# Two score blocks and two value blocks in one TensorE step: a change to an attention + feed-forward kernel

## The chip, the cores and the metric

The kernel runs on one core of one Trainium2 chip. The metric is the device time of one execution in microseconds (us); lower is better. Three runs of the kernel before the change are given, and one execution of it was profiled.

## The reference

Attention with eight heads over 8 batches of 576 positions, then a feed-forward layer. Half of the heads see a window of the last 32 positions (local), the other half see every 32nd position (strided). All is float32.

```python
scores = scale * np.matmul(q, k.transpose(0, 1, 3, 2))          # (8, 8, 576, 576), head_dim 64
mask_local   = (rel >= 0) & (rel < 32)                           # heads 0..3
mask_strided = (rel >= 0) & (pos[None, :] % 32 == pos[:, None] % 32)   # heads 4..7
scores = np.where(masks[None], scores, -1000000000.0)
attn = softmax(scores)
x = np.matmul(attn, v)            # to (4608, 512)
h = x @ w_in                      # (4608, 2048)
g = h * (1.0 / (1.0 + np.exp(-1.702 * h)))
out = g @ w_out                   # (4608, 512)
```

## The kernel before, in words

**The feed-forward part.** Each product of `x` with `w_in` is made from float32r pieces: a value is split into a high and a low part, and high·high, high·low and low·high are added, which gives six matmuls of 128x128 weights on 288 columns for one product (two halves of the contraction, three pairs). Batch 0 is multiplied plainly, four outputs of two units for each of eight weight tiles (`plain`, L451). Batches 1 to 7 use seven products for eight (`product`, L470; `combine`, L484, adds them up on ScalarE and VectorE and stores the result to DRAM). One product of weight tile n and kind k goes to one of six PSUM banks: `mx`, `my`, `mz`, one set for even and one for odd n. After the last batch a second stage reads the hidden values back, applies the gate and multiplies by `w_out`; it isn't touched by the change.

**Steps and sides.** The program is recorded in steps of one product each (the loop at L834). A pass is one batch: 56 steps (8 weight tiles, 7 products each), and the first pass, `plain`, has 64 units. Every other piece of work is put behind a numbered step with `side(step, function, ...)`; all engines keep the order in which it was recorded. So a table of step numbers decides what stands where in each engine's queue.

**Attention of the next batch runs inside a pass.** A batch's attention is cut into six pairs of blocks (`_pairs`, L57), three local ones ("l") and three strided ones ("s"); from batch 1 on they alternate s, l. Batch 0's six pairs come before everything else. For batch b + 1, the loop at L621 puts into pass b, for each pair: `scores` (L215: TensorE, small matmuls, into the two banks `s0` and `s1`), `masked` (L265, VectorE, out of these banks), `maxima` (VectorE), `below` (GpSimd), `exps` (ScalarE), `totals` (VectorE), `scaled` (GpSimd), `turn` (L311: four TensorE transposes into `s0`, and a ScalarE copy out of it), `values` (L321: TensorE, small matmuls into `s0` and `s1`, and at once the copies out of them). `scores` and `values` are a TensorE step of their own between two products, so there are twelve such steps in a pass, and seven passes that hold them. All pairs use the same two banks one after the other. In the TensorE array the small matmuls sit in parts: scores of an l pair in parts of 64 rows by 32 columns, scores of an s pair and values of either kind in parts of 64 by 64. A profile row names a matmul's weights in that way (`64*32`, `64*64`; `54*64` is the values of an s pair, whose 54 rows lie in a part of 64).

**Weights.** `w_in` comes in as 64-bit words; `w_scale`, `w_low`, `w_join`, `w_high` and `w_low_part` (L397 to L422) make the high and low parts of a tile, then `t_load`, `t_sums`, `t_high` and `t_low` (L429 to L443) the sums of its quarters that the seven products need. They are put behind steps of the first passes (L636 to L647).

**Batch 1's input** is made from batch 1's values by `x_sum`, `x_high` and `x_low` (L367 to L385) just before the first product that uses it, by the table at L605.

Of the kernel before, what the change touches and what calls it, by code (L numbers as in the profile page):

```python
# [9 lines left out]
F32 = mybir.dt.float32  # L10
# [16 lines left out]
U = 2  # L27
# [43 lines left out]
def attn_ffn(ctx, tc, qk, vs, weights, masks, ident, out):  # L71
# [143 lines left out]
    def scores(p, banks):  # L215
# [14 lines left out]
        for i in range(4):  # L230
            for q0, n, k0, nk in windows(kind):
                for j in range(2):
                    rows = slice(j * D, (j + 1) * D)
                    matmul(
                        banks[j][q0 : q0 + n, i * WL : i * WL + nk],
# [7 lines left out]
    def parts_of(p, banks):  # L243
# [6 lines left out]
            bank[:nq, : 4 * WL].rearrange("p (i n) -> p i n", i=4)[:, :, :nk] for bank in banks  # L250
# [14 lines left out]
    def masked(p, banks):  # L265
        nq, nk, mask, pr, heads, srcs, (nmax, _, _) = parts_of(p, banks)
# [54 lines left out]
    def values(p, banks, shared=False):  # L321

# [5 lines left out]
        for g in range(2):  # L328
            for w, (q0, n, _, nk) in enumerate(windows(kind)):
                if kind == "s":  # L330
                    n = min(n0, (w + 1) * WS) - w * WS
                for u in range(U):
                    i = U * g + u
                    o = g * n0 + (q0 if kind == "l" else w * WS)
                    for j in range(2):
# [3 lines left out]
                            banks[u][j * D : (j + 1) * D, o : o + n],  # L339
                            lhsT=v[rows, i, w, :], rhs=pt[rows, i * nq + q0 : i * nq + q0 + n],  # L340
                            start=True, stop=True,
                        )
        x = {k: xr[k].rearrange("p (g n) -> p g n", g=2) for k in ("11", "12", "21", "22")}
        for u in range(U):
            src = banks[u][:, : 2 * n0].rearrange("p (g n) -> p g n", g=2)
            copy = vector.tensor_copy if shared and u else scalar.copy
            if kind == "l":
                h, o = divmod(c + u, 3)
                copy(out=x[("11", "21")[h]][:, :, o * QL : (o + 1) * QL], in_=src)
                continue  # L350
            n, r0, half = RES[c], R0[c + u], NPOS // 2
            src = src.rearrange("p g (r t) -> p g t r", r=n)
            for k, h in enumerate(("12", "22")):
                o = x[h].rearrange("p g (t r) -> p g t r", r=STRIDE)[:, :, :, r0 : r0 + n]
                copy(out=o, in_=src[:, :, k * half : (k + 1) * half])
# [76 lines left out]
    def t_sums(i):  # L432
        b11, b21, b22, b12 = (t_view(0)[:, q] for q in range(4))
        t1, t2, t3, t4 = (t_view(1 + i % 2)[:, q] for q in range(4))
        for o, x, y in ((t1, b12, b11), (t2, b22, t1), (t3, b22, b12), (t4, b21, t2)):
            gpsimd.tensor_tensor(out=o, in0=x, in1=y, op=ALU.subtract)
# [10 lines left out]
    six = [m_banks[i][x] for x in ("mx", "my", "mz") for i in range(2)]  # L447
# [516 lines left out]
```

## Time and profile before

| | |
|---|---|
| median of three runs | 859.72 us (858.7 to 861.0) |
| profiled execution | 858.98 us |
| its span, first to last instruction | 857.0 us |
| TensorE busy | 838.0 us, 98% |
| VectorE, ScalarE, GpSimd busy | 549.7, 426.9, 490.9 us |
| mean granted TensorE clock | 0.993 |

The difference between the profiled execution and its span, 1.98 us, lies around the program. In the trace all instructions have the line of one helper (L87), so one tells them by their tiles: `mx`, `my`, `mz` and `s` are PSUM banks, `xa` holds the split input, `w` the split weights, `arena` all else. PE is TensorE, PEld its weight loads, DVE VectorE, ACT ScalarE, POOL GpSimd. `128*128 128x288` are the weights and the output of a matmul. A row of a timeline gives the start, the length, the instruction and how often it follows itself; the lengths of matmuls overlap, so the distance of two starts is what a piece of work takes.

### The profile page before, as it was taken

What the parts mean: (1) busy time and instruction counts of PE and PEld (TensorE: products, weight loads), DVE (VectorE), ACT (ScalarE), POOL (GpSimd) and SP (SyncE); (2) the same over time, 40 slices, a digit from 0 to 9 for tenths busy, and PEclk for the clock granted to TensorE, in tenths of its full rate; (3) what the DMA queues carried; (4) which work ended last, traced back from release to release, by engine and by line L of the source; (5) the groups of instructions that cost most, each with busy time, mean ns of one, the idle gap of its engine ahead of it and who ended that gap; (6) DMA issues with size and microseconds to landing.
All of it is one profiled execution on the core that took longest, in us unless ns stands there. A gap on an engine that the chain in (4) does not pass through costs nothing. (4 is left out here: it accounts for less than half of the span.)

```text
span 857.0 us, 23992 instructions
## 1 busy us (share of the span) xinstructions
PE 838.0 (98%) x9827; PEld 808.8 (94%) x9827; DVE 549.7 (64%) x867; ACT 426.9 (50%) x666; POOL 490.9 (57%) x509
## 2 busy tenths in 40 slices
PE   7899999999999999999999999999999999999997
PEld 4799898999999999999999999999999999999997
DVE  5575776965857658558577775665565565566662
ACT  4675444433444434434446564655555655655540
POOL 2233866242332342423344358999998998777760
PEclk9999999999999999999999999999999999999999
DMA  8897576576685765766768853444433433443430
GB/s 330 289 395 282 174 234 222 164 254 210 205 265 175 242 212 189 253 215 203 223 233 259 266 195 109 152 159 127 146 123 124 146 126 124 141 131 123 136 106 31
DMA packets 112239, 164.84 MB, mean 192 GB/s; under 512 B 9729, under 2 KB 88321, under 8 KB 111105
## 3 DMA queue, kind: packets, MB, share of 16 engines
q1 hardware_dynamic: 112128, 163.31, 58.5%
q8 instruction: 77, 1.26, 0.6%
q14 instruction: 34, 0.27, 0.1%
HBM read 104.55 MB, written 58.72 MB: 191 GB/s over the span
## 5 line engine op out<-in xcount | busy, mean ns | idle before, releaser
L87 POOL TENSOR_TENSOR arena<-arena 128x256 f32<-128x256 f32 (+1 forms) x302 | 332.3, 1117 | 127.3 <-ACT arena L87 54.5
L87 DVE TENSOR_TENSOR xa<-arena,xa 128x576 fp32r<-128x576 f32 (+2 forms) x100 | 158.8, 1589 | 87.6 <-ACT xa L87 56.4
L87 PE MATMUL my<-xa,w 128*128 128x288 f32 x1140 | 180.3, 300 | 0.5 <-DVE arena L87 0.4
L87 ACT ACTIVATE arena<-arena 128x1024 f32<-128x1024 f32 (+2 forms) x120 | 105.4, 878 | 125.7 <-DMA arena<-hid 93.7
L87 PEld LDWEIGHTS my<-xa,w 128*128 128x128 f32 x1140 | 158.7, 189 | 3.3 <-DVE arena L87 1.0
L87 ACT CAST xa<-arena 128x576 fp32r<-128x576 f32 (+2 forms) x102 | 115.5, 1147 | 38.2 <-PE s L87 25.1
L87 PE MATMUL mx<-xa,w 128*128 128x288 f32 x804 | 132.0, 301 | 2.5 <-DVE w L87 1.0
L87 PE MATMUL mz<-xa,w 128*128 128x288 f32 x792 | 128.4, 300 | 0.0
L87 ACT COPY arena<-mx 128x288 f32<-128x288 f32 (+1 forms) x136 | 53.7, 395 | 143.0 <-PE mx L87 107.9
L87 PEld LDWEIGHTS mx<-xa,w 128*128 128x128 f32 x804 | 113.5, 190 | 4.9 <-DVE w L87 1.3
L87 DVE TENSOR_TENSOR arena<-my,arena 128x288 f32<-128x288 f32 (+1 forms) x204 | 90.0, 446 | 41.0 <-PE my L87 39.3
L87 PEld LDWEIGHTS mz<-xa,w 128*128 128x128 f32 x792 | 110.9, 188 | 1.5
L87 POOL TENSOR_TENSOR arena<-arena,rinv 96x512 f32<-96x512 f32 (+1 forms) x48 | 49.5, 1031 | 107.6 <-DVE rinv L87 64.3
L87 DVE TENSOR_TENSOR arena<-mz,arena 128x288 f32<-128x288 f32 (+1 forms) x166 | 71.7, 441 | 51.8 <-PE mz L87 50.0
L87 ACT COPY arena<-s 128x90 f32<-128x90 f32 (+4 forms) x184 | 51.3, 340 | 82.5 <-PE s L87 82.1
L87 DVE TENSOR_TENSOR ga<-arena,ga 128x1792 fp32r<-128x1792 f32 (+1 forms) x25 | 57.4, 2297 | 51.6 <-ACT ga L87 40.6
L87 POOL TENSOR_TENSOR arena<-arena,nmax 128x432 f32<-128x432 f32 (+1 forms) x42 | 46.3, 1103 | 76.7 <-DVE nmax L87 72.7
L87 PE MATMUL mz<-w_out,xa 128*128 128x256 f32 x576 | 75.5, 280 | 0.0
L87 PE MATMUL mx<-w_out,xa 128*128 128x256 f32 x576 | 75.4, 280 | 0.0
L87 PE MATMUL my<-w_out,xa 128*128 128x256 f32 x576 | 75.3, 280 | 0.0
L87 PEld LDWEIGHTS mx<-w_out,xa 128*128 128x128 f32 x576 | 71.1, 188 | 0.0
L87 PEld LDWEIGHTS my<-w_out,xa 128*128 128x128 f32 x576 | 71.0, 188 | 0.0
(72 smaller groups left out, 1000.8 us busy)
## 6 DMA issues: line engine op xcount, KB each, us to landing
hid<-arena SPq DMA_DIRECT2D x256, 144.0 KB, 3.2
arena<-hid SPq DMA_DIRECT2D x144, 256.0 KB, 3.3
arena<-qk SPq DMA_DIRECT2D x23, 448.0 KB, 4.5
arena<-qk SPq DMA_DIRECT2D x21, 472.0 KB, 4.4
arena<-vs SPq DMA_DIRECT2D x23, 384.0 KB, 4.6
out<-arena SPq DMA_DIRECT2D x34, 256.0 KB, 2.9
raw<-w_in SPq DMA_DIRECT2D x8, 1024.0 KB, 10.1
stage<-w_out SPq DMA_DIRECT2D x16, 512.0 KB, 5.1
```

Source lines behind the costliest of these rows:

```text
L87: ins = call(*args, **kw)
```

## The change

The scores of two pairs and the values of the two pairs ahead of them now stand in one TensorE step, without a product between them; there are four such steps in a pass, of which the first has only scores and the last only values.

- The scores of the second pair go to columns 256 and up of `s0` and `s1` (argument `at`), those of the first to columns 0 to 255.
- The values go to two other banks, `v_banks`: `mx` of odd weight tiles and `mz` of even ones, the second pair's from column 216 on. These banks belong to the products too; the steps are placed where both stand empty between two uses. The copies out of them are recorded behind the step, for the first bank's two pairs ahead of the second's (`moved`).
- `turn` uses `s0` for the first pair and `s1` for the second.
- `plain` uses four banks in place of six, since the two of `v_banks` are taken.
- `w_low_part` runs on GpSimd in place of VectorE for all weight tiles but the first, and weight tiles 2 to 7 are made every 6 steps instead of every 7.
- `t_sums` is cut into four pieces, one a step, and starts 5 steps earlier.
- Batch 1's input pieces are made in another order, and its first two products are exchanged (`early_one`): kind 1 ahead of kind 0. From batch 2 on, the sums start one step later.

```diff
+        return lambda u: moved(p, u, banks[u][:, at : at + 2 * n0], shared)
...
     def w_low_part(i):
-        vector.tensor_tensor(out=lo, in0=words[i], in1=hi.bitcast(F32), op=ALU.subtract)
+        (gpsimd if i else vector).tensor_tensor(
+            out=lo, in0=words[i], in1=hi.bitcast(F32), op=ALU.subtract
+        )
...
-    six = [m_banks[i][x] for x in ("mx", "my", "mz") for i in range(2)]
+    four = [m_banks[0]["mx"], m_banks[0]["my"], m_banks[1]["my"], m_banks[1]["mz"]]
+    v_banks = [m_banks[1]["mx"], m_banks[0]["mz"]]
...
-        bank = six[1 + 2 * f if j >= 4 * FP - 2 else j % 6][:, :HALF]
+        bank = (v_banks[0] if j == 4 * FP - 4 else four[j % 4])[:, :HALF]
...
+    def block(p, q, moves):
+        for i in range(2):
+            if q is not None:
+                scores(q + i, s_banks, 256 * i)
+                load_qk(q + i + 2)
+        for i in range(2):
+            if p is not None:
+                moves[i] = values(p + i, v_banks, p < 2 * PAIRS, 216 * i)
+                load_v(p + i + 2)
+
+    def blocks_of(b, slots):
+        for g in range(4):
+            s, q = slots[g], b * PAIRS + 2 * g
+            moves = {}
+            side(s, block, q - 2 if g else None, q if g < 3 else None, moves)
+            if g:
+                for i in range(4):
+                    side(s, lambda i=i, m=moves: m[i % 2](i // 2))
+            if g == 3:
+                break
+            for i in range(2):
+                p, last = q + i, slots[g + 1]
+                side(s + i, masked, p, s_banks, 256 * i)
+                for f, d in ((maxima, 2), (below, 2), (exps, 5), (totals, 6), (scaled, 6)):
+                    side(s + d + i * (2 if f in (totals, scaled) else 1), f, p, s_banks)
+                side(last - ((3, 2) if b == 1 else (3, 1))[i], turn, p, s_banks[i])
...
-        for i in range(PAIRS if b + 1 < B else 0):
...
-            side(s + t[3], turn, p, s_banks[0])
-            side(s + t[4], values, p, s_banks)
-            side(s + t[4], load_v, p + 2)
+        if b + 1 < B:
+            blocks_of(b + 1, [at + t for t in ((3, 16, 30, 44) if b else (3, 18, 33, 48))])
...
-        at = 7 * (i - 2) + 4
+        at = 6 * (i - 2) + 4
...
-        at = HEAD - 10 + STEP * i
-        for t, f in ((-3, t_load), (0, t_sums), (6, t_high), (8, t_low)):
+        at = HEAD - 15 + STEP * i
+        for m in range(4):
+            side(at + m, t_sum, i, m)
+        for t, f in ((-3, t_load), (6, t_high), (9, t_low)):
...
-                    product(n, k)
-                    combine(n, k)
+                    early_one = n == FP and k < 2
+                    product(n, 1 - k if early_one else k)
+                    if early_one and k == 0:
+                        continue
+                    for m in range(2) if early_one else (k,):
+                        combine(n, m)
```

What this does to TensorE's queue, in the middle of a pass of a late batch. `mx_76`, `my_77`, `mz_78` are the banks of even weight tiles, `mx_79`, `my_80`, `mz_81` of odd ones, `s_82` and `s_83` the two score banks; output `64x54` are an s pair's scores, or, with `x2`, its values (`64x36 x2` too), `32x64` an l pair's scores, `64x32 x2` an l pair's values. Before:

```order
L87 MATMUL my_80<-xa,w_757 128x288 x6
L87 MATMUL s_82<-arena 64x54 x2
...
L87 MATMUL mx_76<-xa,w_874 128x288 x6
L87 MATMUL s_82<-arena 64x54
...
L87 MATMUL mz_81<-xa,w_757 128x288 x6
...
L87 MATMUL s_82<-arena 64x32 x2
...
L87 MATMUL my_77<-xa,w_874 128x288 x6
L87 MATMUL s_82<-arena 32x64
...
L87 MATMUL mx_79<-xa,w_993 128x288 x6
```

After, a step with all four blocks, the transposes and the product ahead of it, and the products behind it up to the next use of `mx_79`:

```order
L87 MATMUL s_83<-ident_sb,arena 128x96 x4
L87 MATMUL my_77<-xa,w_666 128x288 x6
L87 MATMUL s_82<-arena 64x54
...
L87 MATMUL s_82<-arena 32x64
...
L87 MATMUL mx_79<-arena 64x54 x2
...
L87 MATMUL mx_79<-arena 64x32 x2
...
L87 MATMUL my_80<-xa,w_550 128x288 x6
L87 MATMUL mx_76<-xa,w_666 128x288 x6
L87 MATMUL mz_81<-xa,w_550 128x288 x6
...
L87 MATMUL mx_79<-xa,w_724 128x288 x6
```

The four blocks that stood alone between products now follow each other, and the values have left the score banks; four products stand between the values and the next product into `mx_79` (the fourth, into `my_77`, is left out above).

GpSimd's queue where the first pass begins (`w_550`, `w_636` or `w_666`, `w_757` or `w_724` are weight tiles 1, 2, 3; `nmax` marks `below`, `rinv` marks `scaled`). Before:

```order
L87 TENSOR_TENSOR arena<-arena,nmax_577 128x4x2x54
L87 TENSOR_TENSOR arena<-arena,rinv_579 128x4x2x54
L87 TENSOR_TENSOR arena<-arena,nmax_671 96x4x128
L87 TENSOR_TENSOR arena<-arena,rinv_673 96x4x128
L87 TENSOR_TENSOR arena<-arena,nmax_784 128x4x2x54
```

After:

```order
L87 TENSOR_TENSOR w_550<-raw_121,w_550 128x4x256
L87 TENSOR_TENSOR arena<-arena,nmax_608 128x4x2x54
L87 TENSOR_TENSOR arena<-arena,nmax_623 96x4x128
L87 TENSOR_TENSOR arena<-arena,rinv_610 128x4x2x54
L87 TENSOR_TENSOR w_666<-raw_534,w_666 128x4x256
L87 TENSOR_TENSOR arena<-arena,rinv_625 96x4x128
L87 TENSOR_TENSOR w_724<-raw_542,w_724 128x4x256
```

The low parts of the weight tiles now stand among the attention work of GpSimd's queue.

More of the change, by code (lines that the diff above doesn't have):

```diff
@@ L213, in geom, with scores @@
         return nq, nk, 1, masks_sb[:nq, m, :nk].unsqueeze(1).broadcast_to([nq, 4, nk])
-    def scores(p, banks):
+    def scores(p, banks, at=0):
         kind = pairs[p][0]
@@ L241, in attn_ffn, with parts_of @@
     sums_of = {}
-    def parts_of(p, banks):
+    def parts_of(p, banks, at=0):
         nq, nk, _, mask = geom(p)
@@ L249, in parts_of @@
         srcs = [
-            bank[:nq, : 4 * WL].rearrange("p (i n) -> p i n", i=4)[:, :, :nk] for bank in banks
+            bank[:nq, at : at + 4 * WL].rearrange("p (i n) -> p i n", i=4)[:, :, :nk]
+            for bank in banks
         ]
@@ L319, in turn, with values @@
         scalar.copy(out=pts[p % 2][:, : 4 * nq], in_=bank[:, : 4 * nq])
-    def values(p, banks, shared=False):
+    def values(p, banks, shared=False, at=0):
         kind, b, c = pairs[p]
@@ L342, in values, with moved @@
                         )
+        return lambda u: moved(p, u, banks[u][:, at : at + 2 * n0], shared)
+    def moved(p, u, src, shared):
+        kind, _, c = pairs[p]
         x = {k: xr[k].rearrange("p (g n) -> p g n", g=2) for k in ("11", "12", "21", "22")}
[L344 to L355, printed above, removed]
+        src = src.rearrange("p (g n) -> p g n", g=2)
+        copy = vector.tensor_copy if shared and u else scalar.copy
+        if kind == "l":
+            h, o = divmod(c + u, 3)
+            copy(out=x[("11", "21")[h]][:, :, o * QL : (o + 1) * QL], in_=src)
+            return
+        n, r0, half = RES[c], R0[c + u], NPOS // 2
+        src = src.rearrange("p g (r t) -> p g t r", r=n)
+        for k, h in enumerate(("12", "22")):
+            o = x[h].rearrange("p g (t r) -> p g t r", r=STRIDE)[:, :, :, r0 : r0 + n]
+            copy(out=o, in_=src[:, :, k * half : (k + 1) * half])
     halves = {k: t.rearrange("p (c n) -> p c n", c=2) for k, t in xr.items()}
@@ L557, in attn_ffn @@
         if i >= 3:
-            values(i - 3, s_banks, i == n0 + 2)
+            move = values(i - 3, s_banks, i == n0 + 2)
+            for u in range(U):
+                move(u)
         if i == 4:
@@ L620, in attn_ffn @@
             side(at, x_sum, 4, b)
-        for i in range(PAIRS if b + 1 < B else 0):
-            p = (b + 1) * PAIRS + i
-            s = at + 4 + 6 * i if b > 1 else at - 3 * b + 7 * i + 2 * (not b)
-            t = (4, 5, 6, 9, 11) if b > 1 else (4, 5, 6, 11, 12) if b and not i else (5, 6, 7, 10, 12)
-            side(s, scores, p, s_banks)
-            side(s, load_qk, p + 2)
-            for f, d in ((masked, 0), (maxima, 1), (below, 2), (exps, t[0]), (totals, t[1]), (scaled, t[2])):
-                side(s + d, f, p, s_banks)
-            side(s + t[3], turn, p, s_banks[0])
-            side(s + t[4], values, p, s_banks)
-            side(s + t[4], load_v, p + 2)
+        if b + 1 < B:
+            blocks_of(b + 1, [at + t for t in ((3, 16, 30, 44) if b else (3, 18, 33, 48))])
     def word(f, i):
@@ L686, in attn_ffn @@
     for h in range(2 * FP):
-        c = first(2 + h // 3) + 9 + 14 * (h % 3) if h < 15 else last - 5
+        c = first(2 + h // 3) + 8 + 14 * (h % 3) if h < 15 else last - 5
         side(c - 8, half_load, h)
```

28 lines of the change are left out of this document (14 added, 14 removed).

## The prediction

> **What bounds the kernel now.** I read the page first, then the stretches by time.
>
> ```profile
> span 857.0 us, 23992 instructions
> PE 838.0 (98%) x9827; PEld 808.8 (94%) x9827; DVE 549.7 (64%) x867; ACT 426.9 (50%) x666; POOL 490.9 (57%) x509
> ```
>
> ```profile
> 240.00:300.00 60.00, 60.00 (x890) 57.16 (x888) 40.14 (x85) 25.93 (x63) 21.06 (x27) 1.00 0.69 220
> 300.00:360.00 60.00, 60.00 (x900) 57.07 (x892) 41.28 (x88) 24.92 (x64) 21.74 (x28) 1.00 0.68 217
> ```
>
> TensorE (PE) is busy for 98% of the span, and in the passes (columns: length, then busy us of PE, PEld, DVE, ACT, POOL, granted clock, DMA share) for all of it, at full clock, with the next engine at two thirds. So the time is what stands in TensorE's queue, and the question is what a row in it costs beyond its own columns. That is read from the distances of starts in TensorE's timeline, in the middle of a pass:
>
> ```profile
> 312.47 0.95 PE L87 MATMUL mx<-xa,w 128*128 128x288 f32 x6
> 313.36 0.67 PE L87 MATMUL s<-arena 54*64 54x54 f32 x32
> 313.96 1.07 PE L87 MATMUL mz<-xa,w 128*128 128x288 f32 x6
> 314.86 0.96 PE L87 MATMUL my<-xa,w 128*128 128x288 f32 x6
> 315.66 0.96 PE L87 MATMUL mx<-xa,w 128*128 128x288 f32 x6
> ...
> 319.29 0.90 PE L87 MATMUL s<-arena 64*64 64x32 f32 x48
> 320.12 1.06 PE L87 MATMUL mx<-xa,w 128*128 128x288 f32 x6
> 321.02 0.96 PE L87 MATMUL mz<-xa,w 128*128 128x288 f32 x6
> ```
>
> A product followed by a product takes 0.80 us from start to start (314.86 to 315.66). A product followed by attention takes 0.89 (312.47 to 313.36), and the first product behind attention 0.90 (313.96 to 314.86). The attention itself, start to next start, takes 0.60 with 32 matmuls and 0.83 with 48 (319.29 to 320.12). The 16 more cost 0.23, so one costs 14.4 ns and 32 cost 0.46; 0.14 of the 0.60 is the way out. A step of attention alone thus has a fixed price of 0.09 + 0.14 + 0.10 = 0.33 us, whatever is in it. In the waits the same shows as weight loads that wait for nothing named:
>
> ```profile
> PEld s L87 <- issue: 12.1, 73, 0.4
> ```
>
> **The change: fewer steps.** There are twelve attention steps in a pass and four after, in seven passes: 8 x 7 = 56 fixed prices fewer, 56 x 0.33 = 18.5 us. The small matmuls themselves stay, and so do the transposes; no engine that TensorE waits for hides this part, since TensorE never waits there.
>
> In place of each step removed stands a join between two blocks. Per pass there is one in the first step (s scores to l scores), three in each of the middle two, one in the last (s values to l values): 8. Three of these join parts of 64 by 64 to parts of 64 by 64 (both of the last kind, in three steps). Five have l scores, in parts of 64 by 32, on one side.
>
> The first kind stands in the trace, before the passes, where scores and values of batch 0 follow each other:
>
> ```profile
> 16.77 0.69 PE L87 MATMUL mx<-early 64*64 64x54 f32 x32 [2.32 <-DMA early<-qk]
> 17.28 0.86 PE L87 MATMUL s<-arena 64*64 64x32 f32 x48
> ```
>
> 0.51 from start to start, against the 0.46 of 32 matmuls: at most 0.05, and some of that belongs to the first block's entry. I take 0.03: 21 x 0.03 = 0.6 us.
>
> The second kind, between 64 by 64 and 64 by 32, stands nowhere in the trace. Its bounds are this cheap join, 0.03, and a whole fixed price, 0.33, since it can't need more than leaving for a product and coming back. [...] 35 x 0.14 = 4.9 us (1.1 to 11.6). [...]
>
> Together: 18.5 - 0.6 - 4.9 = 13.0 us less in TensorE's queue.
>
> **The change: new waits in the passes.** Three could arise.
>
> *Scores behind the second transpose.* The second pair's transposes are one product ahead of the next scores, which overwrite the same bank, so its copy must be out.
>
> ```profile
> 317.24 0.50 PE L87 MATMUL s<-ident_sb,arena 96*128 96x96 f32 x4
> 317.52 1.84 PE L87 MATMUL my<-xa,w 128*128 128x288 f32 x12
> ```
>
> ```profile
> 283.55 0.60 PE L87 MATMUL s<-ident_sb,arena 128*128 128x128 f32 x4
> ```
>
> ```profile
> 284.18 0.59 ACT L87 COPY arena<-s 128x512 f32<-128x512 f32 x1 [1.05 <-PE s L87]
> ```
>
> ```profile
> L87 ACT COPY arena<-s 128x384 f32<-128x384 f32 x21 | 10.1, 480 | 26.6 <-PE s L87 26.6
> ```
>
> ScalarE starts the copy 0.03 us after the transposes' end (284.15 to 284.18). For an l pair that is 0.50 + 0.03 + 0.48 = 1.01 us from their start. TensorE reaches the scores after 0.28 (317.24 to 317.52) and one product with its way in, 0.89: 1.17. A margin of 0.16 us, so no wait as long as ScalarE is free; what stands ahead of the copy is a copy of a product two earlier. I take 0 here; 0.1 in each of 14 steps would be 1.4 us.
>
> *Products behind the values.* The values lie in product banks. Each step's six copies stand together in ScalarE's queue; the first bank has to be free after four products, 4 x 0.80 + 0.10 = 3.3 us.
>
> ```profile
> L87 ACT COPY arena<-s 128x90 f32<-128x90 f32 x62 | 10.3, 259 | 9.0 <-PE s L87 9.0
> L87 ACT COPY arena<-s 128x192 f32<-128x192 f32 x48 | 13.0, 323 | 27.6 <-PE s L87 27.6
> ```
>
> Its three copies take 2 x 0.26 + 0.32 = 0.84 us: 2.4 us to spare, with ScalarE busy for 25 of 60 us. Cost 0.
>
> *VectorE's queue.* `masked` now waits for both pairs' scores, and the next sums of products stand behind it. While it waits TensorE is at the values, and the bank those sums empty is next written four products later. Cost 0.
>
> **The change: the first pass and its end.** TensorE stands still in a few places before; these rows give the idle time in brackets.
>
> ```profile
> 43.49 0.66 PE L87 MATMUL s<-ident_sb,arena 128*128 128x128 f32 x4 [0.29 <-POOL arena L87]
> ```
>
> ```profile
> 95.09 0.40 PE L87 MATMUL mx<-xa,w 128*128 128x288 f32 x1 [0.74 <-ACT xa L87]
> 96.24 0.93 PE L87 MATMUL mx<-xa,w 128*128 128x288 f32 x5 [0.75 <-DVE xa L87]
> ```
>
> ```profile
> 144.19 0.55 PE L87 MATMUL s<-ident_sb,arena 96*128 96x96 f32 x4 [1.05 <-POOL arena L87]
> ```
>
> At 95 and 96 the first product of batch 1 waits for its input, which ScalarE and VectorE make late. After the change the kind that is needed first is made first, and kind 0 has two more steps: I take both away, 1.5 us. At 43.5 and 144.2 a transpose waits for GpSimd, at 144 behind four of the weight sums in a row; these now stand one a step, and the transposes later behind their `scaled`: 0.3 gone, and half of 1.05, 0.5, since GpSimd has no less to do.
>
> Against that, weight tile 1's low part goes to GpSimd.
>
> ```profile
> L87 POOL TENSOR_TENSOR xa<-arena,xa 128x576 fp32r<-128x576 f32 x2 | 2.8, 1416 | 3.6 <-ACT xa L87 3.6
> ```
>
> ```profile
> 37.00 1.23 DVE L87 TENSOR_TENSOR w<-raw,w 128x1024 fp32r<-128x1024 f32 x1 [1.12 <-ACT w L87]
> ```
>
> ```profile
> 38.21 1.75 PE L87 MATMUL mz<-xa,w 128*128 128x288 f32 x12
> 39.89 0.74 PE L87 MATMUL s<-arena 64*32 64x64 f32 x48
> 40.55 1.86 PE L87 MATMUL mz<-xa,w 128*128 128x288 f32 x12
> ```
>
> The same subtraction on GpSimd takes 1.416 x 1024 / 576 = 2.5 us, in place of 1.23: from 37.0 to 39.5. TensorE needed the tile at 38.21, as VectorE ended; now the second pair's scores (0.66, 39.89 to 40.55) stand ahead of that, so it comes at 38.87 and waits 0.6 to 0.7. I take 0.7. For tiles 2 to 7 the lead grows by two steps a tile, since they are made every 6 steps and used every 8: cost 0. The four banks of `plain` are used again after 8 steps in place of 12, and hold a result for 3 of them; 5 products, 4 us, cover the copy. Together: 0.7 - 1.5 - 0.3 - 0.5 = -1.6 us.
>
> **The sum.** 13.0 + 1.6 = 14.6 us off the profiled execution's 858.98 (span 857.0 and 1.98 around it). That execution lies 0.74 below the median, 859.72; from the median: 845.1 us.
>
> **The rivals.**
>
> *Joins of 64 by 64 with 64 by 32 are free.* They cost 0.03 like the others: 18.5 - 56 x 0.03 + 1.6 = 18.4 us, 841.3. For it: 48 l scores take 0.66 to the next product (39.89 to 40.55), less than 48 values, so the smaller parts as such cost nothing. Against it: the way in and out of the full array shows that a change of shape can cost.
>
> *They cost a whole fixed price.* 35 x 0.33 = 11.6: 18.5 - 0.6 - 11.6 + 1.6 = 7.9, 851.8. For it: the price of a change in the trace is the same for every block. Against it: 0.19 of it belongs to the 288-column neighbours.
>
> *GpSimd late in the first pass.* If low parts of tiles 1 to 7 keep TensorE waiting 2 us each in place of 0.7 once, 13.3 us more, and the sum is nearly nil: 858.4.
>
> ```profile
> 0.00:60.00 60.00, 50.59 (x958) 41.09 (x959) 37.05 (x76) 36.38 (x69) 20.06 (x34) 0.97 0.89 332
> ```
>
> For it: seven times 2.5 us put among `below` and `scaled`, whose results the transposes need. Against it: POOL is busy for a third of the first 60 us, and the lead grows.
>
> *Slower: products wait for ScalarE to empty the value banks.* ScalarE's queue is in order; if a copy or an `exps` ahead of the six waits, all six wait, and the next product into `mx` with them. It decides from a lateness of 2.4 us, and to eat 14.6 us in 21 such steps it must be 0.7 more, 3.1 each time. At 4 us each: 21 x 1.6 = 33.6, so 878.7. For it: ScalarE waits for GpSimd and DMA in places. Against it: an `exps` stands 5 steps behind its scores, and the next value step 8 behind that.
>
> **How the numbers follow.** The forecast has 0.55, free joins 0.20, joins at full price 0.13, GpSimd late 0.07, slower 0.05. 0.3% of 859.72, 2.6 us, is about what a measurement can tell from no change; faster means below 857.1. The first three and about half of the fourth are faster: 0.92; the other half of the fourth, 0.03, is within; slower 0.05. The forecast's own range is 842 to 848; taking in free joins (841.3, with the stalls all gone down to 839) and full price (851.8, with 1.4 of scores waiting for a copy up to 853) gives 839 to 853.
>
> **What would show it.** In the profile after: the weight loads that wait on "issue" at `s` drop from 73 to about a third; a step with all four blocks takes 160 x 14.4 ns = 2.3 us, plus two joins of 0.14 and one of 0.03 and the way out 0.14, some 2.8 us to the next product; no idle brackets at steps of scores or at `mx` of odd tiles in the passes; about 0.7 us idle for POOL at the first `w` product of tile 1; none at batch 1's first product. Wrong would be: a gap over 0.3 us at l scores, `mx` or `s` waiting on ACT in each pass, or PE no longer busy at 60 of 60 us in the passes.

## The result, and the profile after

| | before | after |
|---|---|---|
| median | 860.36 us (4 runs, 858.70 to 861.14) | 866.15 us (4 runs, 862.45 to 867.74) |
| profiled execution, its span | 858.98, 857.0 us | 862.45, 860.7 us |
| TensorE busy | 838.0 us | 827.9 us |
| granted clock of the four runs after | | 0.993 (profiled), 0.984, 0.984, 0.990 |

The ratio is 1.0066, with a 95% interval of 1.0043 to 1.0089: the kernel is slower by 5.7 us, where 14.6 less was forecast. TensorE's own work did shrink, by 10 us. The page:

```profile
span 860.7 us, 23887 instructions
PE 827.9 (96%) x9827; PEld 806.5 (94%) x9827; DVE 539.4 (63%) x869; ACT 422.3 (49%) x657; POOL 501.3 (58%) x516
```

So 33 us of the span are idle for TensorE in place of 19. Where, the stretches by time tell (length; busy us of PE, PEld, DVE, ACT, POOL; granted clock; DMA share; GB/s):

```profile
120.00:180.00 60.00, 55.46 (x793) 53.57 (x794) 40.14 (x82) 23.88 (x57) 27.82 (x30) 0.97 0.63 197
240.00:300.00 60.00, 60.00 (x914) 58.74 (x907) 41.80 (x90) 25.07 (x66) 21.40 (x28) 1.00 0.71 230
360.00:420.00 60.00, 58.14 (x860) 56.58 (x859) 41.35 (x85) 24.11 (x60) 22.59 (x28) 1.00 0.66 219
```

TensorE is full in one pass and not in the next, though all passes hold the same work. For the account, the span is cut at fixed products (each 56th product starts a pass), and the starts are read from the trace:

| stretch | before | after | change |
|---|---|---|---|
| up to the first product | 28.42 | 27.97 | -0.45 |
| first pass, with the first products of batch 1 among its last | 71.00 | 74.17 | +3.17 |
| batch 1's pass | 58.93 | 65.79 | +6.86 |
| passes of batch 2, 3, 4, 5 | 57.40 each | 56.00, 56.05, 55.40, 55.98 | -6.16 |
| pass of batch 6 | 57.40 | 58.26 | +0.86 |
| batch 7 and the second stage | 411.66 | 411.05 | -0.61 |

**What came as forecast.** A pass in which TensorE waits for nothing takes 55.40 in place of 57.40. The 2.0 us stand against 13.0 / 7 = 1.86 forecast. In TensorE's timeline, a step of four blocks and the products around it:

```profile
292.48 1.04 PE L87 MATMUL my<-xa,w 128*128 128x288 f32 x6
293.45 1.35 PE L87 MATMUL s<-arena 64*64 64x54 f32 x80
...
295.87 0.23 PE L87 MATMUL mx<-arena 64*64 64x32 f32 x2
295.88 0.23 PE L87 MATMUL mz<-arena 64*64 64x32 f32 x2
296.03 1.07 PE L87 MATMUL my<-xa,w 128*128 128x288 f32 x6
```

It takes 2.58 us from its start to the next product (293.45 to 296.03), where 2.8 was expected. Inside it, the first matmul behind a join of s and l scores starts 148 ns after the last one ahead of it, and 146 ns between l scores and s values; neighbours of one kind mostly stand 6 to 39 ns apart, the last s value and the first l value 20 ns. (Three neighbours inside blocks stand 47 to 80 ns apart.) So a join of the second kind costs some 0.11 us, 148 less 38 ns (forecast 0.14), and one of the first kind nothing that can be seen (forecast 0.03). The weight loads that wait for "issue" at `s` fall from 73 to 16:

```profile
PEld s L87 <- issue: 3.2, 16, 0.5
```

**What had not been forecast.** TensorE's waits (us in total, times, the longest):

```profile
PE s L87 <- POOL arena L87: 5.4, 8, 2.2
PE my L87 <- ACT w L87: 4.5, 1, 4.5
PE my L87 <- issue: 1.9, 2, 1.5
PE mz L87 <- issue: 1.8, 1, 1.8
PE mx L87 <- issue: 1.5, 1, 1.5
PE mx L87 <- POOL w L87: 0.2, 1, 0.2
```

The last line is the wait for weight tile 1, forecast at 0.7 and 0.2 in fact. The other five come to some 15 us, of which 1.5 (transposes for GpSimd) stood there before; they have three causes. One wait outside these lines is a kind that the prediction had named: in the first pass, scores wait for ScalarE's copies of the transposes out of `s0` and `s1`.

```profile
66.05 0.97 ACT L87 COPY arena<-s 128x512 f32<-128x512 f32 x2
66.70 1.00 PE L87 MATMUL s<-arena 64*64 64x54 f32 x29 [0.81 <-ACT arena L87]
```

*Batch 1's first products.* Where two waits of 0.74 and 0.75 were to vanish, there is one of 4.53:

```profile
91.90 1.75 PE L87 MATMUL my<-xa,w 128*128 128x288 f32 x12
98.18 1.06 PE L87 MATMUL my<-xa,w 128*128 128x288 f32 x3 [4.53 <-ACT w L87]
```

GpSimd's timeline after and, below it, before. `sums` are the weight sums, `arena` 128x576 is `x_sum` 3, batch 1's input:

```profile
83.68 2.94 POOL L87 TENSOR_TENSOR sums<-sums 128x256 f32<-128x256 f32 x4 [3.33 <-issue]
91.39 0.73 POOL L87 TENSOR_TENSOR sums<-sums 128x256 f32<-128x256 f32 x1 [4.77 <-DMA sums<-plains]
92.08 1.43 POOL L87 TENSOR_TENSOR arena<-arena 128x576 f32<-128x576 f32 x1
```

```profile
86.49 3.35 POOL L87 TENSOR_TENSOR sums<-sums 128x256 f32<-128x256 f32 x4 [4.93 <-DMA sums<-plains]
89.80 1.43 POOL L87 TENSOR_TENSOR arena<-arena 128x576 f32<-128x576 f32 x1
94.03 1.54 POOL L87 TENSOR_TENSOR sums<-sums 128x256 f32<-128x256 f32 x2 [2.81 <-DMA sums<-plains]
```

Before, `x_sum` 3 stands behind tile 0's sums and ahead of tile 1's. After, the first of tile 1's sums is one step ahead of it, and waits 4.77 us for its load (there is one landing buffer, free only when tile 0's sums are made at 86.6). `x_sum` 3 stands behind it with its input ready, and ScalarE's queue behind that:

```profile
94.84 0.67 ACT L87 CAST xa<-arena 128x576 fp32r<-128x576 f32 x1 [5.46 <-DVE arena L87]
...
97.08 1.05 ACT L87 CAST w<-sums 128x1024 fp32r<-128x1024 f32 x1 [0.70 <-POOL sums L87]
```

*Transposes that wait for GpSimd*, 2.15 and 0.81 in batch 1's pass and 0.31 in most others. In GpSimd's queue the two `below` and the two `scaled` of a group stand among the weight sums:

```profile
115.95 0.66 PE L87 MATMUL s<-ident_sb,arena 128*128 128x128 f32 x4 [2.15 <-POOL arena L87]
```

```profile
107.74 5.11 POOL L87 TENSOR_TENSOR arena<-arena,nmax 128x432 f32<-128x432 f32 x2 [1.20 <-DVE nmax L87]
112.81 2.22 POOL L87 TENSOR_TENSOR sums<-sums 128x256 f32<-128x256 f32 x3
114.99 0.91 POOL L87 TENSOR_TENSOR arena<-arena,rinv 128x432 f32<-128x432 f32 x1
```

The first `scaled` ends at 115.9, and the transposes start with it. The order is not all of it: the two `below` take 5.11 us (2.09 and 3.06), where the other groups of this pass need 0.92 and 1.04. The long ones, from 107.74 to 112.85, run while VectorE subtracts the low parts of `xa` and `w` (three subtractions between 107.88 and 111.94, of 0.74, 1.29 and 1.21 us); that this is the reason was not tested.

*Waits on "issue" at steps of four blocks*, four of them, 5.1 us in all: 1.46 at 123.3 and 1.83 at 141.5 inside a step, 1.54 at 409.9 and 0.31 at 425.7 in the product right behind one. TensorE, in the middle of the values of an l pair:

```profile
121.58 0.23 PE L87 MATMUL mx<-arena 64*64 64x32 f32 x2
121.59 0.23 PE L87 MATMUL mz<-arena 64*64 64x32 f32 x2
123.28 0.25 PE L87 MATMUL mx<-arena 64*64 64x32 f32 x2 [1.46 <-issue]
123.30 0.25 PE L87 MATMUL mz<-arena 64*64 64x32 f32 x2
```

No engine, semaphore or transfer of data is named. The page has a queue for instructions:

```profile
q8 instruction: 77, 1.26, 0.6%
```

77 packets of 16 KB for the 19,711 TensorE instructions of the trace come to 256 instructions a packet, an estimate from these two counts that takes all the packets for TensorE's. Counted in the program, all four stalls lie at the same place modulo 256, instruction 226 or 227 (192 or 193 if the trace's are counted); I take this place for the cut between two such blocks. For the stall at 123.28 the packet started at 120.94, 1.66 us into the step, took 0.99 us, and TensorE went on 2.34 us after its start. The same holds for every wait on issue at such a cut in the passes of the changed kernel and of the experiments below, 33 in all: TensorE goes on 2.2 to 2.9 us after a packet of this queue starts. That TensorE waits there for the next instructions themselves is my theory, the "instruction fetch" of the expectations below; the traces show the places and the times. A four-block step is 160 matmuls with a weight load each, 320 instructions in 2.5 us, so it can meet two cuts within 2 us, less than these 2.2 to 2.9. The steps that stall start at 180, 173, 162 and 155 (modulo 256, from the program's start; the expectations below call this instructions into a block), 46 to 71 ahead of a cut, and meet the next one 302 to 327 instructions in, at their end or a few instructions behind it. Eight of the ten others end before their second cut. Two start 2 and 9 instructions ahead of the first, so that the second lies inside the step too; for them the packet starts 0.9 and 1.1 us ahead of the step, some 3 us before the second cut, and there is no wait. A step before had at most 96 instructions.

### The profile page after: what moved, and what is told of

It reads as the page before. It is cut to its first block, busy times and chain, and to the rows that moved or that the text cites. A ratio compares the mean times of both kernels' runs of the same rounds, so it can differ in the third digit from the quotient of the medians.

```text
span 860.7 us, 23887 instructions
## 1 busy us (share of the span) xinstructions
PE 827.9 (96%) x9827; PEld 806.5 (94%) x9827; DVE 539.4 (63%) x869; ACT 422.3 (49%) x657; POOL 501.3 (58%) x516
## 5 line engine op out<-in xcount | busy, mean ns | idle before, releaser
L87 POOL TENSOR_TENSOR arena<-arena 128x256 f32<-128x256 f32 (+1 forms) x302 | 323.8, 1089 | 145.8 <-ACT arena L87 67.8
L87 PE MATMUL my<-xa,w 128*128 128x288 f32 x1200 | 190.2, 300 | 8.2 <-ACT w L87 4.5
L87 PEld LDWEIGHTS my<-xa,w 128*128 128x128 f32 x1200 | 167.8, 190 | 10.5 <-ACT w L87 4.7
L87 ACT ACTIVATE arena<-arena 128x1024 f32<-128x1024 f32 (+2 forms) x120 | 104.1, 878 | 123.3 <-DMA arena<-hid 94.4
L87 ACT COPY arena<-mx 128x288 f32<-128x288 f32 (+4 forms) x201 | 67.0, 358 | 183.7 <-PE mx L87 126.1
L87 PE MATMUL mx<-xa,w 128*128 128x288 f32 x768 | 126.6, 300 | 1.2 <-DVE w L87 1.0
L87 PE MATMUL mz<-xa,w 128*128 128x288 f32 x768 | 124.1, 298 | 0.0
L87 PEld LDWEIGHTS mx<-xa,w 128*128 128x128 f32 x768 | 109.5, 190 | 2.4 <-DVE w L87 1.2
L87 POOL TENSOR_TENSOR arena<-arena,nmax 128x432 f32<-128x432 f32 (+1 forms) x42 | 50.8, 1218 | 98.9 <-DVE nmax L87 91.6
L87 DVE TENSOR_TENSOR ga<-arena,ga 128x1792 fp32r<-128x1792 f32 (+1 forms) x25 | 55.4, 2215 | 52.2 <-ACT ga L87 34.8
L87 PEld LDWEIGHTS mz<-w_out,xa 128*128 128x128 f32 x576 | 70.9, 188 | 0.0
```

Source lines behind the costliest of these rows:

```text
L87: ins = call(*args, **kw)
```

## The experiments

All kernels are the changed one or the one before, with the edit shown; the ratio is always to the kernel before, measured beside it.

### 1. Batch 1's third sum one step earlier

```
-  (-8, x_sum, 1), (-7, x_sum, 3), (-6, x_sum, 2)
+  (-8, x_sum, 1), (-8, x_sum, 3), (-6, x_sum, 2)
```

> The changed kernel with one number moved: batch 1's x_sum of kind 3 goes one step earlier, so that in GpSimd's queue it stands ahead of the first piece of weight tile 1's sums and no longer behind it. Theory 'queue order': that piece waits 4.8 us for its DMA and holds up x_sum, and with it batch 1's first product, so the 4.5 us wait of TensorE at 98 us goes, and the kernel takes 861 to 862 us against 866 of the changed kernel (before: 860). Rival 'GpSimd has too much to do in the first pass': its work is the same, the wait only moves to the next product, and the time stays at 865 to 866.

863.6 us, ratio 1.0033 (1.0012 to 1.0054). TensorE's timeline:

```profile
94.91 1.04 PE L87 MATMUL my<-xa,w 128*128 128x288 f32 x6 [0.62 <-DVE arena L87]
...
107.11 0.40 PE L87 MATMUL my<-xa,w 128*128 128x288 f32 x1 [2.55 <-ACT xa L87]
108.47 0.85 PE L87 MATMUL my<-xa,w 128*128 128x288 f32 x2 [0.96 <-DVE xa L87]
```

The wait of 4.53 falls to 0.62: the place in GpSimd's queue was its cause. But of the 3.9 us, 2.5 come back twelve microseconds later, where other parts of the same input are late: 3.5 in place of the 1.03 that the changed kernel waits there. The wait of 2.15 for GpSimd is gone; the two `below` ahead of it now take

```profile
105.37 2.43 POOL L87 TENSOR_TENSOR arena<-arena,nmax 128x432 f32<-128x432 f32 x2
```

in place of 5.11 us. The first pass and batch 1's pass together take 136.7 us in place of 140.0. The time lies between theory (861 to 862) and rival (865 to 866). The four waits on issue stay at the same steps (1.46, 1.56, 1.50, 0.06).

### 2. The weight sums where they stood before

```
-  at = HEAD - 15 + STEP * i
-  for m in range(4): side(at + m, t_sum, i, m)
+  at = HEAD - 10 + STEP * i
+  for m in range(4): side(at, t_sum, i, m)
```

> The changed kernel with the weight sums as before the change: the four pieces of a tile at once, five steps later. Theory 'queue order': the 4.5 us at 98 us go, and so do most of the waits behind them for GpSimd (1.0 at 110, 2.2 at 116, 0.8 at 133 us), since a tile's sums wait for the DMA into one landing place that the sums before them must have left, and pieces spread over steps leave it later; 857 to 860 us. Rival 'GpSimd has too much to do': low parts of the weights still stand in its queue, so over 3 us of waits for POOL stay in the first two passes and the time is 862 or more.

869.47 us, ratio 1.0098 (1.0065 to 1.0130). The theory failed: TensorE now waits 4.59 for ScalarE and 2.70 for the weights of batch 1's first products. In GpSimd's queue `x_sum` 3 now stands behind all four sums of tile 0, which wait for their load until 91.45. So the earlier place of the sums is not in itself what costs the time.

### 3. Other places in the blocks of 256

The warm-up's first 7 matmuls of 512 columns become 72 of 48: 130 instructions more ahead of everything, the columns nearly the same.

```
-  fill(FILL[i][0], late)
+  for _ in range(72):
+      matmul(late[:, :48], lhsT=zeros[:, :P], rhs=zeros[:, :48], start=True, stop=True)
```

> The changed kernel with 65 more matmuls (130 more TensorE instructions) in the warm-up at the start: 72 of 48 columns in place of 7 of 512, so that nothing changes but where the program's instructions are cut into fetches of 256. Theory 'instruction fetch': a step of four blocks is 320 instructions in 2.5 us, and where it begins some 25 to 85 instructions ahead of a cut it runs through the whole next fetch before the one after it has landed; with the shift no step begins there but one or two at the edge, and the 5.1 us of waits for 'issue' at 123, 141, 410 and 426 us go (at most 1 us in all stays, near 182, 197 or 349 us); 861 us against 866. Rival 'the steps themselves wait' (a bank, a semaphore that the profile does not show): the waits stay at the same four steps and the time at 866.

868.93 us, ratio 1.0098 (1.0065 to 1.0132): the 861 of the theory did not come. No wait on issue is left at the four steps; they now come at 186.6 and 204.4, in the pass behind, and one at 57.9 among plain products:

```profile
183.79 0.23 PE L87 MATMUL mx<-arena 64*64 64x32 f32 x2
186.65 0.25 PE L87 MATMUL mz<-arena 64*64 64x32 f32 x2 [2.63 <-issue]
```

The steps with a wait start at 204 and 197; the old ones did at 180, 173, 162 and 155. The place is as the fetch theory says; the size is not: 2.63 and 1.18, and 1.08 at 57.9, where at most 1 in all was expected. And batch 1's pass, now without its waits on issue of 3.3 us, takes 64.2, only 1.6 less, since the transposes wait for GpSimd instead, 2.15, 2.65 and 1.37 in three groups in place of 2.15, 0.81 and none. In that pass two things are late, one behind the other.

### 4. A product between scores and values

```
-  side(s, block, ...)            # scores and values
+  side(s, block_s, ...)
+  side(s + 1, block_v, ...)      # one product later
```

> The changed kernel with a product between the scores and the values of each step of four blocks: six steps a pass, none over 160 instructions. Theory 'instruction fetch': no wait for 'issue' in the passes, 5.1 us less; 14 more steps at 0.33 less a join of 0.12 each cost 2.9 us: 864 against 866. Rival 'the steps themselves wait': the waits move to the steps of values, and the time is 868 to 869.

864.37 us, ratio 1.0056 (1.0030 to 1.0083). The expected 864 came out, but not by the expected way: the waits on issue do not vanish, they become 0.43, 0.78, 1.12 and 0.19, 2.5 us in place of 5.1. A later pass takes 0.3 to 0.4 more. The wait of 4.5 at batch 1's first product stays, and those for GpSimd at transposes of batch 1's pass grow from 3.0 to 5.1. The time can't be told from that of the changed kernel.

### 5. Grouped steps from batch 2's pass on, all else as before

Kernel before, with `block` and `blocks_of` of the change for the passes of batch 2 to 6:

```
+  if 1 < b < B - 1:
+      blocks_of(b + 1, [at + t for t in (3, 16, 30, 44)])
-  for i in range(PAIRS if b + 1 < B else 0):
+  for i in range(PAIRS if b < 2 else 0):
```

> The kernel before, with the grouped steps of the change only from the pass of batch 2 on; the first pass and the pass of batch 1 are those of before. Theory one (the loss sits in the first pass and in the pass of batch 1, in the order of GpSimd's queue, and the grouped steps bring what they should, 1.4 us a pass with the wait for GpSimd at a pass's first transposes): five passes of 55.99 us in place of 57.40, so 7.0 us fewer, less about 1.5 us each for the two grouped steps that now start 187 and 180 instructions into a block of 256 (last pass with attention): some 856 us, 3 to 5 below before, and no wait over 1.1 us at batch 1's first product. Rival (the grouped steps as such are what costs, by banks, by a late ScalarE or by the clock): five passes no shorter than 57.4, 860 or more.

857.77 us, ratio 0.9968 (0.9951 to 0.9984): faster than before. The five passes take 55.40, 55.98, 56.77 (with 0.52 on issue), 55.98 and 60.13. The first has no wait for GpSimd at its transposes, so 0.31 us of that wait makes 0.6 us of a pass. The last has its two steps at 187 and 180, with waits of 2.54 and 1.13:

```profile
403.91 0.24 PE L87 MATMUL mz<-arena 64*64 64x32 f32 x2 [2.54 <-issue]
```

### 6. The side work of the change alone

Kernel before, with the change's order of weights, weight sums and batch 1's parts (the last four hunks of the diff), and its low parts on GpSimd; attention stays one block a step.

```
-  at = 7 * (i - 2) + 4
+  at = 6 * (i - 2) + 4
...
-  for t, f in ((-3, t_load), (0, t_sums), (6, t_high), (8, t_low)):
+  for m in range(4): side(at + m, t_sum, i, m)      # at is five steps earlier
+  for t, f in ((-3, t_load), (6, t_high), (9, t_low)):
```

> The kernel before with the side work of the change alone: weight tiles every 6 steps, low parts of tiles 1 to 7 on GpSimd, weight sums five steps earlier and one piece a step, batch 1's parts in the new order; attention stays one block a step. Theory one (queue order on GpSimd is the cause): batch 1's first product waits 4 us or more, as after the change, the first pass and the pass of batch 1 together take 6 to 10 us more than before, the later passes 57.4 each: 866 to 870. Rival (the grouped attention of the first two passes makes the inputs late): no wait over 1.1 us at batch 1's first product, 858 to 861.

861.45 us, ratio 1.0024 (1.0008 to 1.0039): far below the 866 of theory one, and 0.45 above the rival's range, which allowed no wait over 1.1. Batch 1's first product waits

```profile
98.20 0.40 PE L87 MATMUL my<-xa,w 128*128 128x288 f32 x1 [0.99 <-ACT xa L87]
100.36 1.01 PE L87 MATMUL my<-xa,w 128*128 128x288 f32 x5 [1.75 <-DVE xa L87]
```

2.7 us, against 1.5 before and 4.5 in the changed kernel; `x_sum` 3 stands behind a weight sum that waits 3.83 us for its load, as after the change. Batch 1's pass takes 58.90 as before. So the order alone takes the gain away that I had put down there and makes a small loss of it; most of the loss came only with grouped attention beside it.

### 7. The sum earlier, and the low parts back on VectorE

```
-  (-8, x_sum, 1), (-7, x_sum, 3)
+  (-8, x_sum, 1), (-8, x_sum, 3)
-  (gpsimd if i else vector).tensor_tensor(
+  vector.tensor_tensor(
```

> The changed kernel with batch 1's third sum one step earlier in GpSimd's queue, and the low parts of weight tiles 1 to 7 back on VectorE. Theory (GpSimd has too much queued in the first pass): 7 x 2.4 us of GpSimd's time go, the waits for POOL at transposes (116, 131, 151 us) and for xa at 107 fall under 0.5 us each, and the time falls 3 to 5 us below the 863.6 of the run with the sum moved alone: 859 to 861. Rival (VectorE is the late engine at the end of the first pass): the waits for DVE at xa grow past 1 us, 863 or more.

864.88 us, ratio 1.0063 (1.0042 to 1.0083), not the 859 to 861 of the theory and no better than experiment 1: the waits for GpSimd at transposes are eleven now, 5.7 us together, and the two for `xa` are 2.95 and 0.96. So seven low parts on GpSimd are not why its results come late. The rival has the time right; the wait for VectorE that it named, over 1 us, stays at 0.96.

### 8. Experiment 5 at another place, and transposes one step later

```
-  side(last - (3, 1)[i], turn, p, s_banks[i])
+  side(last - ((2, 1) if g == 0 else (3, 1))[i], turn, p, s_banks[i])
+  118 warm-up matmuls of 30 columns in place of 7 of 512
```

> As the kernel with grouped steps from batch 2's pass on, with two edits more: the first group's transposes one step later for its first pair, which should take away the wait of 0.31 us for GpSimd, worth 0.6 us a pass; and 111 matmuls of 30 columns more in the warm-up in place of 7 of 512, which move all later instructions by 222, so that the ten grouped steps start 65, 58, 215, 208, 109, 102, 3, 252, 153 and 146 instructions into a block. Theory (a step that starts some 155 to 205 into a block overtakes the fetch): no wait on issue over 0.4 us but perhaps one of up to 1 at 208; five passes of 55.4: 850 us, 9 to 10 below before. Rival (waits on issue belong to the last grouped pass, not to the place in the block): two of about 1.5 us at 410 and 426 us as in the changed kernel, 853 or more.

855.34 us, ratio 0.9946 (0.9926 to 0.9966). 850 us were expected. The waits for GpSimd in the grouped passes are gone, and passes without a wait on issue take 55.4 to 55.5, as expected. The two waits left the last pass's two steps, as expected too; but two came elsewhere, 1.73 in the step that starts at 208, and 1.84 some products behind the one at 153. Each is followed by a lower granted clock. Ahead of the first wait, around it, and behind it:

```profile
244.00:247.00 3.00, 1.86 (x118) 1.60 (x111) 0.78 (x3) 0.00 (x0) 0.00 (x0) 1.00 0.84 252
247.00:252.00 5.00, 4.40 (x40) 4.36 (x40) 1.62 (x4) 1.49 (x7) 0.62 (x1) 0.66 0.72 257
252.00:256.00 4.00, 4.00 (x32) 4.00 (x32) 2.66 (x7) 2.08 (x5) 1.34 (x2) 1.00 0.50 188
```

A clock of 0.66 over 5 us is 3.4 us at half speed, 1.7 us lost; half speed is what the clock shows after the change, 0.50 from 142.5 to 145.9. So this pass takes 59.01, 3.6 more than 55.4: 1.73 of wait and 1.7 of clock.

### 9. No grouped step between 143 and 208

As 8, with 124 matmuls in the warm-up (of 28 columns, to keep their sum; 234 instructions more than experiment 5), and a product between scores and values in the last pass alone, whose steps would start at 165 and 158.

```
+  apart = int(b == B - 1 and 0 < g < 3)
+  side(s, block, None if apart or not g else q - 2, q if g < 3 else None, moves)
+  if apart: side(s + 1, block, q - 2, None, moves)
```

> Grouped steps from batch 2's pass on, the first pair's transposes one step later in the first group, and two edits against the waits on issue: 117 matmuls of 30 columns more in the warm-up in place of 7 of 512 (all later instructions move by 234), so that the grouped steps start 77, 70, 227, 220, 121, 114, 15 and 8 instructions into a block, outside the 143 to 208 where waits were seen; in the last pass with attention, where they would start at 165 and 158, a product stands between scores and values, as in the run with all steps split. Theory (place in the block of 256): no wait on issue in the first four of the five passes, 55.4 us each; about 1.3 us of waits and 0.3 for the split in the last, so 10.0 - 1.6 = 8.4 us below before, 850 to 852.5. Rival (the waits come in some pass or other whatever the place): two of 1.5 us or more, and a slower clock behind them, as with 111 matmuls: 855.

853.03 us, ratio 0.9913 (0.9891 to 0.9934): the fastest kernel here, 7 us below before, where 8.4 was expected. In the eight unsplit grouped steps there is no wait on issue; the first four grouped passes take 55.40, 55.76, 55.47 and 55.47, with TensorE full:

```profile
220.00:280.00 60.00, 59.98 (x874) 58.64 (x874) 44.01 (x90) 25.42 (x64) 23.38 (x28) 1.00 0.70 228
280.00:340.00 60.00, 60.00 (x878) 58.77 (x877) 44.12 (x92) 26.41 (x66) 24.02 (x30) 1.00 0.67 221
```

In the last, 59.74, the split did not help. A clock at half speed for 3.4 us, from 402.5 on (the product at 402.49 takes 1.42 us to the next start, where 0.80 is usual), adds 1.7 us to this wait:

```profile
401.36 0.24 PE L87 MATMUL mx<-arena 64*64 64x32 f32 x1 [1.55 <-issue]
```

### 10. The changed kernel, batch 1's pass alone ungrouped

```
-  if b + 1 < B:
+  if b + 1 < B and b != 1:
       blocks_of(...)
+  # for b == 1: the loop of before, one block a step
```

> The changed kernel, with the pass of batch 1 alone back to one block a step (its slots of before); the first pass and passes 2 to 6 stay grouped, the side work stays that of the change. Theory (grouping in that pass costs 6.9 us: two fetch waits of 1.5 and 1.8, two waits for GpSimd at transposes of 2.2 and 0.8, the rest of it clock and late parts): the pass takes 59 to 60.5 in place of 65.8, the wait of some 4.5 us at batch 1's first product stays, and so do about 3 us of waits on issue in the last pass with attention: 859 to 861.5. Rival (the late inputs of batch 1 delay the pass whatever is in it): the pass 63 or more, 864 or more.

860.72 us, ratio 1.0003 (0.9984 to 1.0023). The pass takes 58.43 in place of 65.79, better than expected, though the late input is still there in front of it:

```profile
100.44 0.89 PE L87 MATMUL my<-xa,w 128*128 128x288 f32 x4 [3.84 <-ACT xa L87]
```

Waits for GpSimd at transposes in that pass come to 0.6 us in place of 3.0, and there are none on issue. The last grouped pass has 2.23 and 1.47 on issue (steps at 171 and 164).

### 11 and 12. The side work in two parts

Kernel before with the low parts of tiles 1 to 7 on GpSimd and nothing else (11), and with all the side work of experiment 6 but that (12).

```
11:
-  vector.tensor_tensor(
+  (gpsimd if i else vector).tensor_tensor(
12: experiment 6 with this line as before
```

> The kernel before with one edit of the change: the low parts of weight tiles 1 to 7 on GpSimd. As predicted, one wait of 0.7 to 0.9 us for tile 1 and nothing else: the first pass 72, 860.5 to 862. Rival (7 x 2.4 us on GpSimd hold up the transposes and the sums of batch 1): the first pass 73.5 or more, with waits for POOL beyond those of before, 863 or more.

859.68 us, ratio 0.9997 (0.9980 to 1.0014), just below the expected 860.5 to 862, and a first pass of 70.50. The wait that was expected is there:

```profile
41.58 0.67 PE L87 MATMUL mz<-xa,w 128*128 128x288 f32 x3 [0.88 <-POOL w L87]
```

> The kernel before with the side work of the change (weight tiles every 6 steps, weight sums earlier, batch 1's parts in the new order) but the low parts left on VectorE. Theory (batch 1's third sum stands behind weight sums that wait for a DMA): the waits at batch 1's first two products come to 2.5 us or more, against 1.5 before, and none for a weight tile at 41 us; 860.5 to 862. Rival (the low parts on GpSimd were what made them late): waits of 1.5 or less, 858.5 to 860.

860.79 us, ratio 1.0009 (0.9992 to 1.0025); waits of 0.96 and 1.76 at batch 1's first products, 2.7 in all, as in experiment 6. Neither part can be told from no change in the time; the wait of 0.9 belongs to the low parts, that of 2.7 to the order.

## Why the prediction was wrong

**The account.** From the ratios: grouping in passes 2 to 6 makes -2.8 us (experiment 5), the side work alone +2.1 (6), the changed kernel without grouping in batch 1's pass +0.3 (10), with it +5.7. The difference of the last two, +5.4, is the price of grouping in batch 1's pass, and what is left, 0.3 + 2.8 - 2.1 = +1.0, that of grouping in the first pass. This adds up by construction, and each term has an uncertainty of 1 to 2 us. Against the forecast, by the stretches of the profiled executions: the passes of batch 2 to 6 are 4.0 us longer than forecast (-5.3 against 5 x -1.86), batch 1's pass 9.2 (+6.86 against -1.86 - 0.5) and the first pass with its end 6.1 (+3.17 against -1.86 - 1.1). That is more than the 18.3 us between -14.6 and +3.7, since the start and the second stage came out 1.1 shorter.

**Fewer steps and joins: right.** 18.5 - 5.5 = 13.0 us was forecast for seven passes, 1.86 each; a clean pass gains 2.0. The prices were near: some 0.11 and 0 a join for 0.14 and 0.03. The 0.14 is the price measured for the way out of a step; no run of before shows it for a join of 64 by 64 with 64 by 32. After the change the starts at those joins stand 146 and 148 ns apart, against 6 to 39 at most others, which gives the 0.11; why they cost this was not shown. Neither the rival of free joins nor that of full-price joins decided anything.

**"New waits in the passes. Three could arise": this step failed.** The three cost nothing in the steady passes: no scores wait for the copy of the transposes in the passes of batch 2 to 6, and VectorE's queue holds up nothing there. The first of them arose once, in the first pass: 0.81 us at 66.7. Its condition, a free ScalarE, does not hold there: ScalarE is at the weights until 65.9 and at the two copies from 66.05 to 67.02. No product in any pass waits for the value banks, so the rival that ended on the slower side named a wait that isn't there. What cost most was not among the three. The prediction priced a step by the distances of TensorE's starts and put waits on issue at nothing: they came to 5.1 us, with 1.7 of half-speed clock (0.50 from 142.5 to 145.9) behind one of them. In the changed kernel and experiments 1 to 3, 5 and 7 to 10 there are 110 unsplit four-block steps. All 23 that start at 155 to 208 have a wait, 0.06 to 2.63 us, inside the step or in the first product behind it; of the other 87 none does. Four of those, which start at 123, 142, 143 and 153, have a wait one to three products behind (1.08, 0.10, 0.52, 1.84). Moving the program's instructions moves the waits (3, 8), and keeping the steps out of that part leaves eight steps without any (9). That is shown. That TensorE waits there for its instructions is not: it is my reading of the 256 instructions a packet and of the packet that starts 2.2 to 2.9 us ahead of TensorE's going on, each time, and no experiment changed the packets themselves.

**The 0.31 for GpSimd in the passes** (0.6 us a pass, four passes, 2.4 us) was missed as well: the argument looked at the banks behind the transposes and not at `scaled` ahead of the first one. One step later it is gone (8).

**"Together: 0.7 - 1.5 - 0.3 - 0.5 = -1.6 us" for the first pass and its end: this step failed too.** The 0.7 was near (0.21 in the changed kernel, 0.88 alone). The 1.5 to be taken away at batch 1's first product became a wait of 4.5: the prediction looked at the order of the parts among themselves, and not at the weight sums that had been moved past them in GpSimd's queue, nor at the load those wait for. Experiment 1 shows that cause, and also that curing it alone brings 2.5 of the 3.9 us back elsewhere. The 0.3 that the first pass's transposes were to lose came the other way: they wait 1.18 for GpSimd, where 0.50 stood before. The transposes behind weight sums wait 3.0 in batch 1's pass, where 1.05 stood before and half of it was to remain: the sums stand one a step now, but the two `below` and two `scaled` of a group have to pass them together, where before each had its own steps. How much of the 3.0 that order makes is open, since the first group's two `below` alone took 3.2 us longer than usual, more than the 2.15 of wait behind them; where they took 2.43 (experiment 1) that wait was gone. The rival "GpSimd late in the first pass" had the right engine and the wrong reason: experiments 7 and 11 show that the low parts are not it.

**What stays open.** In batch 1's pass the waits named come to 3.3 on issue and 4.0 for GpSimd and the input, less the 1.05 of before; half-speed clock costs 1.7 (at 142) against 0.8 before (the end of a stretch from 97.6 to 101.0), and 2.0 is the gain: 5.2 of the 6.86 us. The rest is not in gaps, of which the profile shows only 0.1 us more in that pass. It may be that a wait costs more than its gap, as the 0.31 at transposes makes 0.6 of a pass. How the price of that pass divides between the waits on issue and GpSimd is not settled: with the 3.3 on issue taken away (3), the waits for GpSimd at transposes grew from 3.0 to 6.2, and the pass became shorter by 1.6, about the 1.7 of half-speed clock that is not in it. How long a stall lasts at the same place of a block goes with when its packet starts: in experiment 5's last pass 2.63 us into the step for the wait of 2.54, and 0.96 for that of 1.13. Why the packet starts early or late was not found out, and so neither why the split in experiment 9 left 1.55 where in experiment 4 it left 0.2 to 1.1.

## What to carry to other kernels

Before many small instructions are put in one run, count them: here a run of 320 instructions in 2.5 us had a wait on issue of 0.06 to 2.63 us, inside it or right behind it, wherever it began 18 to 71 ahead of a cut between blocks of 256 (23 of 23), and one such wait could take back what a pass had gained. Where work is moved in an in-order queue, look at every instruction it now stands ahead of, and at what it itself waits for: one weight sum of 0.7 us that waits 4.77 us for a load held up batch 1's whole input. And change a steady stage before a crowded one: the same grouping that gains 2 us in each steady pass lost 5 in the pass in which GpSimd also makes the weight sums, by late inputs and waits on issue together.

## What the hardware showed that I had not expected

- A wait of TensorE of 1.5 to 2.6 us, in or behind a step of small matmuls, can be followed by 3.4 us at half speed (after the change a granted clock of 0.50 from 142.5 to 145.9, behind the wait of 1.83; experiment 8, twice, 0.66 over 5 us), which costs 1.7 us more and about doubles its price. In all traces, 9 of the 16 waits on issue of over 1.4 us in the passes were followed by it, two of them by 6.8 us (experiments 2 and 10), and none of the 17 shorter ones. Not each long one is: behind the 2.54 of experiment 5 the clock stayed full, and so it did, at 1.00, behind the 1.46 and 1.54 after the change.
- Executions of the same kernel differ by their clock: the four of the changed kernel have 0.993, 0.990, 0.984 and 0.984, and the profiled one, 862.45 us, is both the fastest and the one with the highest. The 3.7 us between the two profiled spans are thus less than the 5.7 between the kernels.
- The start-up has its own scatter: in the profiled executions the first product of batch 0 starts at 27.2 to 29.9 us or at 30.8 to 31.9. The later ones are those in which the clock stays at half for 17 us or, in experiment 9, 10 (from 12 to 34 us the mean granted clock is 0.61 in experiments 5 and 11, 0.92 in 12); the edits don't explain it, since experiments 11 and 12, whose start-up is that of before, show one each (30.8 and 28.6).
